# Four x tiles transposed ahead of the key weights, two more by DMA transpose, and small work moved out of the way, in a gated mix of linear attention and a token MLP

## The chip, the cores and the metric

The kernel runs on one core of a Trainium2 chip. The metric is the device time of one execution in microseconds (us); lower is better. A profiled execution also has a *span*, from its first to its last instruction; the time is the span plus about 2 us. Engine names in the profile: PE is TensorE (matmuls), PEld its weight loads, DVE is VectorE, ACT is ScalarE, POOL is GpSimd, SP is SyncE, which here only issues DMAs. A "q" behind a name means the sequencer of that engine, which issues its DMAs.

## The reference, cut to what matters

```python
x = A_x                                    # 1 x 2048 x 512, bf16
g = sigmoid((x * gate_w).sum(-1))
# a: linear attention with 32 heads of 16
q, k, v = split(x @ wqkv); pk = phi(k); pq = phi(q)      # phi(t) = t+1 if t>0 else exp(t)
kv = einsum("bhsd,bhse->bhde", pk, v);  z = pk summed over s
a = (pq @ kv) / (pq @ z) @ wo
# b: an MLP over the 2048 tokens, one for each channel
h = layernorm(x); u = gelu(h^T @ w1 + b1); b = (u @ w2 + b2)^T
out = g * a + (1 - g) * b
```

## The kernel before

A tile is 128 of the 2048 tokens; there are 16. A matmul contracts over partitions, so the key product of a tile needs x of the tile transposed (`xT`), in four chunks of 128 channels, and the four chunks of Wk. The values are never formed: each tile adds x<sup>T</sup> phi(k) to four accumulators (`gacc`), which are multiplied by Wv once at the end.

The parts that matter here, with cuts marked by `...`:

```python
load_x(nc.sync, 0, 1);  load_x(nc.scalar, 1, 1)          # x tiles 0 and 1
load_wk(nc.sync, 0);    load_wk(nc.scalar, 1)            # chunks of Wk, 128 KB each
load_wk(nc.sync, 2);    load_wk(nc.scalar, 3)
load_x(nc.sync, 2, 2);  load_x(nc.sync, 4, 4);  ...      # the other x tiles
for c in range(2, NSC):                                  # tiles 8 to 15 also transposed by DMA
    nc.sync.dma_start(out=xT[..c..], in_=X[..c..], transpose=True)
...
nc.gpsimd.dma_start(out=brow[...], ...)                  # two biases, and gw_b
...
transpose_tile(0, False); transpose_tile(1, False)       # TensorE, copied out by DVE
warm_up(2, 256)
ln_stats(0); ln_stats(1)
k_tiles((0, 1), lambda: (transpose_tile(2, False), transpose_tile(3, True)))
for t in range(2, NT):
    k_tiles((t,))                       # 4 matmuls; exp on ACT; two DVE steps give pk
    if 4 <= t + 2 < 8:
        transpose_tile(t + 2, True)     # copied out by ACT
    g_tile(t - LAG)                     # 4 matmuls into gacc, LAG = 2
    ...                                 # LayerNorm statistics of tile t on DVE
...                                     # z: 16 small matmuls
for t in range(NT):                     # second phase: first MLP product and the queries
    ...  uacc matmuls (3)  ...  q_block(t)
    if t == 1: biases()                 # transpose of 30 rows on TensorE
    if t == 4: kv_matmuls()
    if t == 8: w2_matmuls()             # 4 matmuls, copied out by DVE
```

PSUM has eight banks, all given out by one pool: four are `gacc`, the rest serve the transposes and the key products. phi takes one step on ACT (exponential) and two on DVE.

## Time and profile before

Median 170.68 us of three executions (170.6 to 170.75). The profile is of a fourth one, which took 171.28 us.

| what | value | view |
|---|---|---|
| TensorE busy | 162.9 of 169.2 us | page, part 1 |
| start of the first matmul of a key product | 4.70 us | timeline of PE |
| start of the first `gacc` | 10.45 us | timeline of PE |
| start of the first `uacc` (end of the key phase) | 37.66 us | timeline of PE |
| four matmuls of one key product or g step, back to back | 0.864 us | chain of waits |
| four transposes, warm | 0.22 us | chain of waits |
| phi of one tile on DVE, start to start | 0.92 us | timeline of DVE |

The first lines of the page: span; busy time of each engine with its share and number of instructions; then two rows in which each digit is the busy share, or the granted clock, of one fortieth of the span, in tenths.

```profile
span 169.2 us, 2119 instructions
...
PE 162.9 (96%) x814; PEld 75.0 (44%) x814; DVE 83.1 (49%) x195; ACT 58.1 (34%) x89; POOL 18.1 (11%) x36
...
PE   7889999999999999999999999999999999999991
...
PEclk9999999999999999999999999999999999999999
...
```

TensorE has nothing to gain but in the first slices. The clock row says full speed.

The timeline of TensorE in the first 14 us (start, duration, engine, line, operation, out<-in, shape, count, and in brackets the idle time before the group and what ended it):

```profile
...
1.26 2.31 PE L109 MATMUL wps<-warm 128*128 128x512 bf16 x5 [1.26 <-DVE ones_f L159]
3.44 1.04 PE L192 MATMUL pt<-ident,xs 128*128 128x128 bf16 x8
...
4.70 1.92 PE L109 MATMUL kacc<-wk_sb,xT 128*128 128x512 bf16 x6
6.96 0.59 PE L109 MATMUL kacc<-wk_sb,xT 128*128 128x512 bf16 x2 [0.34 <-DMA wk_sb<-in_A_wqkv_dram]
7.60 0.62 PE L192 MATMUL pt<-ident,xs 128*128 128x128 bf16 x8
8.51 1.04 PE L109 MATMUL kacc<-wk_sb,xT 128*128 128x512 bf16 x4 [0.29 <-DVE xT L198]
...
10.45 1.04 PE L109 MATMUL gacc<-pk,xs 128*128 128x512 bf16 x4 [0.68 <-DVE pk L206]
...
```

The key products of tiles 0 and 1 start at 4.70 us, wait for the last chunk of Wk (6.96), are followed by the transposes of tiles 2 and 3 (7.60), whose copy ends a wait (8.51), and g(0) waits for phi on DVE (10.45). The chain of waits for the same stretch (start, duration, what) links them:

```profile
...
1.73 5.18 DMA wk_sb<-in_A_wqkv_dram
...
7.60 0.64 PE pt L192 x8
...
8.26 0.60 ACT xT L196
...
9.70 0.70 DVE pk L206
...
```

The only other gap of TensorE lies in the second phase, right behind the four matmuls of W2:

```profile
...
52.49 1.03 PE L109 MATMUL wps<-wo_sb,kvbdT 128*128 128x512 bf16 x4
53.35 0.81 PE L109 MATMUL uacc<-hs,w1c 128*128 128x512 bf16 x3
54.39 1.02 PE L109 MATMUL qacc<-xT,wq_sb 128*128 128x512 bf16 x4 [0.23 <-DVE pqT L206]
...
```

The duration of a group includes about 0.16 us of pipeline behind its last matmul. Three `uacc` matmuls take 0.65 us to issue, so PE stands from 54.00 to 54.39, 0.39 us; the figure in brackets, 0.23, is the same wait counted from the modelled end of the last matmul.

### The profile page before, as it was taken

Reading aid. Unit: us, or ns where it says so; the run is one execution under the profiler, and the core shown is the slowest. Engines: PE = TensorE matmul, PEld = TensorE weight load, DVE = VectorE, ACT = ScalarE, POOL = GpSimd, SP = SyncE. Lnnn points to the kernel's source line nnn. Section 1 sums busy time; section 2 is a strip of 40 time slices with the busy share of each in tenths; the row PEclk is TensorE's granted clock in tenths of the full one; section 3 lists DMA queues with packets and bytes.
Section 4 is the critical chain, followed back from the end, with each engine's and each line's share of the span. In section 5 each row is a group of like instructions: output and inputs, shape, how many; then the busy total and the mean of one; then the engine's idle time right before and its main releaser. Section 6 shows DMA issues by size and latency. Waiting matters only on the chain.

```text
span 169.2 us, 2119 instructions
## 1 busy us (share of the span) xinstructions
PE 162.9 (96%) x814; PEld 75.0 (44%) x814; DVE 83.1 (49%) x195; ACT 58.1 (34%) x89; POOL 18.1 (11%) x36
## 2 busy tenths in 40 slices
PE   7889999999999999999999999999999999999991
PEld 3345444434544444444444444444444444444461
DVE  1679999739899868997013311316112221111121
ACT  3065767682424757222111311006111122211110
POOL 7102020200002000001522341100000000000000
PEclk9999999999999999999999999999999999999999
DMA  5999999999100000660399389971100000110001
GB/s 158 311 233 212 358 349 347 348 349 311 41 0 2 0 0 4 209 225 0 99 308 262 97 277 251 305 228 69 66 33 31 31 31 31 37 59 33 31 31 31
DMA packets 27865, 24.52 MB, mean 145 GB/s; under 512 B 5648, under 2 KB 27280, under 8 KB 27856
## 3 DMA queue, kind: packets, MB, share of 16 engines
q1 hardware_dynamic: 25984, 21.63, 43.7%
q0 software_dynamic: 1440, 2.38, 5.4%
q10 hardware_dynamic: 432, 0.39, 0.7%
q8 instruction: 6, 0.10, 0.2%
q14 instruction: 3, 0.02, 0.0%
HBM read 21.11 MB, written 2.23 MB: 138 GB/s over the span
## 4 chain that ended last, share of the span: by engine, by line
PE 92%; DMA 3%; DVE 1%; ACT 1%; ACTq 1%; issue 0%
PE yps L109 29%; PE uacc L109 28%; PE gacc L109 8%; PE qacc L109 8%; PE aps L109 8%; PE kacc L109 7%; DMA wk_sb<-in_A_wqkv_dram 3%; PE pt L192 1%; PE zacc L109 1%; ACT e L202 1%; PE denps L109 1%; PE kvps L109 1%; DVE pqT L206 0%; DVE pk L206 0%; DVE e L203 0%; ACT xT L196 0%
## 5 line engine op out<-in xcount | busy, mean ns | idle before, releaser
L109 PE MATMUL uacc<-hs,w1c 128*128 128x512 bf16 x224 | 51.3, 379 | 0.0
L109 PE MATMUL yps<-uT,w2c 128*128 128x512 bf16 (+1 forms) x238 | 51.0, 366 | 0.0
L109 PEld LDWEIGHTS <-w2c 128*128 128x128 bf16 x238 | 23.3, 98 | 25.3
L109 PEld LDWEIGHTS <-w1c 128*128 128x128 bf16 x224 | 21.6, 98 | 26.2 <-issue 0.7
L446 DVE SCALAR_TENSOR_TENSOR ot<-yps,c,a_sc 128x512 bf16<-128x512 f32 (+1 forms) x17 | 12.1, 719 | 39.5 <-PE yps L109 38.4
L431 ACT ACTIVATE a_sc<-aps,c,gg 128x512 f32<-128x512 f32 x16 | 12.2, 776 | 46.9 <-PE aps L109 36.3
L395 DVE TENSOR_TENSOR pqT<-pqT,rex 128x512 bf16<-128x512 bf16 x16 | 6.7, 424 | 28.3 <-DMA rex<-rd_dram 28.3
L308 ACT ACTIVATE uT<-uacc,bcol 128x512 bf16<-128x512 f32 x14 | 9.3, 687 | 28.6 <-PE uacc L109 28.6
L109 PE MATMUL kacc<-wk_sb,xT 128*128 128x512 bf16 x64 | 16.8, 384 | 0.7 <-DMA wk_sb<-in_A_wqkv_dram 0.3
L109 PE MATMUL gacc<-pk,xs 128*128 128x512 bf16 x64 | 16.3, 379 | 0.7 <-DVE pk L206 0.7
L109 PE MATMUL qacc<-xT,wq_sb 128*128 128x512 bf16 x64 | 16.4, 379 | 0.2 <-DVE pqT L206 0.2
L109 PE MATMUL aps<-W2sb,pqT 128*128 128x512 bf16 x64 | 16.4, 379 | 0.0
L202 ACT ACTIVATE e<-qacc 128x512 bf16<-128x512 f32 x16 | 9.6, 597 | 14.9 <-PE qacc L109 14.0
L238 ACT ACTIVATE hs<-xs,nmr,rstd 128x512 bf16<-128x512 bf16 x16 | 12.7, 804 | 0.4 <-DMA wv_sb<-in_A_wqkv_dram 0.4
L203 DVE TENSOR_SCALAR e<-e 128x512 bf16<-128x512 bf16 x32 | 9.1, 286 | 6.2 <-ACT e L202 6.0
L202 ACT ACTIVATE e<-kacc 128x512 bf16<-128x512 f32 x16 | 9.3, 597 | 7.5 <-PE kacc L109 7.5
L393 POOL DMA_DIRECT2D rex<-rd_dram x16 | 9.4, 594 | 18.0 <-DVE pqT L395 15.4
L206 DVE SCALAR_TENSOR_TENSOR pk<-kacc,e 128x512 bf16<-128x512 f32 x16 | 11.1, 692 | 0.6
L206 DVE SCALAR_TENSOR_TENSOR pqT<-qacc,e 128x512 bf16<-128x512 f32 x16 | 11.1, 691 | 0.6
L222 DVE BATCH_NORM_STATS2 stats<-xs 128x6 f32<-128x512 bf16 x16 | 10.9, 682 | 0.0
L109 PEld LDWEIGHTS <-xT 128*128 128x128 bf16 x64 | 6.2, 99 | 8.6 <-issue 1.0
L381 DVE CUSTOM_DVE_ANT_0 junk<-xs,gw_b 128x512 bf16<-128x512 bf16 x16 | 9.9, 683 | 0.0
(66 smaller groups left out, 69.1 us busy)
## 6 DMA issues: line engine op xcount, KB each, us to landing
w2c<-in_B_w_dram SPq DMA_DIRECT2D x4, 1792.0 KB, 12.2
w1c<-in_B_w_dram SPq DMA_DIRECT2D x2, 2048.0 KB, 16.9
w1c<-in_B_w_dram SPq DMA_DIRECT2D x3, 1024.0 KB, 10.2
rex<-rd_dram POOLq DMA_DIRECT2D x16, 128.0 KB, 6.7
out_dram<-ot SPq DMA_DIRECT2D x15, 128.0 KB, 1.7
xs<-in_A_x_dram SPq DMA_DIRECT2D x3, 512.0 KB, 7.6
wq_sb<-in_A_wqkv_dram SPq DMA_DIRECT2D x1, 512.0 KB, 4.3
wv_sb<-in_A_wqkv_dram SPq DMA_DIRECT2D x1, 512.0 KB, 11.1
```

What stands on the lines that cost most here:

```text
L109: nc.tensor.matmul(o, lhsT=lhsT, rhs=rhs, start=start, stop=stop, **kw)
L202: nc.scalar.activation(out=e[:], in_=acc[:], func=ACT.Exp)
L203: nc.vector.tensor_scalar(out=e[:], in0=e[:], scalar1=1.0, scalar2=PHI_EPS, op0=ALU.min, op1=ALU.add)
L206: nc.vector.scalar_tensor_tensor(out=dst, in0=acc[:], scalar=0.0, in1=e[:], op0=ALU.max, op1=ALU.add)
L222: nc.vector.bn_stats(out=stats[:], in_=xs[:, t, :])
L238: nc.scalar.activation(out=hs[:, t, :], in_=xs[:, t, :], func=ACT.Identity, scale=rstd[:, t : t + 1], bias=nmr[:, t : t + 1],)
L308: nc.scalar.activation(out=uT[:, j, :], in_=acc[:], func=ACT.Gelu_apprx_tanh, bias=bcol[:, j : j + 1])
L381: nc.vector.tensor_tensor_reduce(out=junk[:], in0=xs[:, t, :], in1=gw_b[:], scale=1.0, scalar=0.0, op0=ALU.mult, op1=ALU.add, accum_out=gp ...
L393: nc.gpsimd.dma_start(out=rex[:], in_=src.unsqueeze(1).to_broadcast([8, HEAD, SC]))
L395: nc.vector.tensor_tensor(out=seg, in0=seg, in1=rex[:], op=ALU.mult)
L431: nc.scalar.activation(out=a_sc[:], in_=aps[:], func=ACT.Identity, scale=gg[:, t : t + 1], bias=c2[:, t : t + 1],)
L446: nc.vector.scalar_tensor_tensor(out=ot[:, :W], in0=yps[:, :W], scalar=c1[:, t : t + 1], in1=a_sc[:, cs], op0=ALU.mult, op1=ALU.add,)
```

## The change

Its intent: let the first four tiles be transposed before any weight is there; then run their key products chunk by chunk, so that each chunk of Wk does four tiles' work as it lands; let the DMA transpose tiles 6 and 7; keep the queues at the start free of small loads; take W2 and its copies off DVE in the second phase. Cut to its core:

```diff
-    load_x 0, 1; load_wk 0..3; load_x 2-3, 4-7, 8-11, 12-15; then xT of 8-11 and 12-15
+    for i in range(2):
+        load_x(nc.sync, 2 * i, 1);  load_x(nc.scalar, 2 * i + 1, 1)
+    for i in range(2):
+        load_wk(nc.sync, 2 * i);    load_wk(nc.scalar, 2 * i + 1)
+    NPE = 6
+    load_x(nc.sync, 4, 2)
+    for t0, n in ((NPE, 2), (8, 4), (12, 4)):
+        load_xT(t0, n)              # DMA transpose
+        load_x(nc.sync, t0, n)
-    nc.gpsimd.dma_start(out=brow..., gw_b...)         # at the start
+    nc.gpsimd.memset(brow[:], 0.0)                    # loads issued at t == 6 of the key phase
-    warm_up(5)            # on a tile that DVE clears first
+    warm_up(6)            # on a constant that is there already
...
+    transpose_tile(0, False); transpose_tile(1, True)
+    warm_up(1, 256)
+    transpose_tile(2, False); transpose_tile(3, True)
+    for k in range(ND - 1):
+        for t in range(HEADS):                        # HEADS = 4
+            k_part(t, (k,))
+    for t in range(HEADS):
+        k_part(t, (ND - 1,))
+        if t == 1:
+            transpose_tile(HEADS, False)
+    for t in range(HEADS):
+        k_phi(t)
+    LAG = 4; LN_LAG = 3; APPLY = 9                    # LAG was 2, APPLY 6; no LN_LAG
+    for t in range(HEADS, NT):
+        k_part(t, range(ND))
+        if t + 1 < NPE:
+            transpose_tile(t + 1, True)
+        k_phi(t); g_tile(t - LAG); ...
+    for t in range(NT - LAG, NT):
+        g_tile(t)
+        if t == NT - 3:
+            for u in range(NT): z_tile(u)             # before: the last z after the last g
-        nc.tensor.transpose(pt[:, 0:n], brow[:], ident[0:n, 0:n])
+        nc.tensor.transpose(pt[:, 0:P], brow[:], ident[:])
-        if t == 8: w2_matmuls()                       # four in a row, copies on DVE
+        elif j <= NB0 + ND: w2_matmul(j - NB0 - 1)    # one after each of four later uacc, copies on ACT
```

More of the change, by code (lines that the diff above doesn't have):

```diff
@@ L92 @@
     gw_b = keep([P, D], BF16, "gw_b")
-    brow = keep([NF + NT, P], BF16, "brow")
+    brow = keep([P, P], BF16, "brow")
     bcol = keep([P, NF + NT], FP32, "bcol")
@@ L105 @@
     ones_f = keep([P, 1], FP32, "ones_f")
-    warm = keep([P, SC], BF16, "warm")
+    warm = nc.const_aps.tensor(1.0, (P, SC), BF16)
     def mm(o, lhsT, rhs, start, stop, **kw):
@@ L128, in load_wk, with load_xT @@
         q.dma_start(out=wk_sb[:, k, :], in_=wqkv_view[:, k, D : 2 * D])
-    load_x(nc.sync, 0, 1)
-    load_x(nc.scalar, 1, 1)
-    load_wk(nc.sync, 0)
-    load_wk(nc.scalar, 1)
-    load_wk(nc.sync, 2)
-    load_wk(nc.scalar, 3)
-    load_x(nc.sync, 2, 2)
-    load_x(nc.sync, 4, 4)
-    load_x(nc.sync, 8, 4)
-    load_x(nc.sync, 12, 4)
-    for c in range(2, NSC):
+    def load_xT(t0, n):
         nc.sync.dma_start(
-            out=xT[:, :, c * SC : (c + 1) * SC], in_=X[c * SC : (c + 1) * SC, :], transpose=True
+            out=xT[:, :, t0 * P : (t0 + n) * P], in_=X[t0 * P : (t0 + n) * P, :], transpose=True
         )
+    for i in range(2):
+        load_x(nc.sync, 2 * i, 1)
+        load_x(nc.scalar, 2 * i + 1, 1)
+    for i in range(2):
+        load_wk(nc.sync, 2 * i)
+        load_wk(nc.scalar, 2 * i + 1)
+    NPE = 6
[3 more added lines that the diff above has]
+        load_x(nc.sync, t0, n)
     nc.sync.dma_start(out=wq_sb[:], in_=wqkv_view[:, :, 0:D])
@@ L156 @@
             nc.sync.dma_start(out=wo_sb[:], in_=wo_view)
-    nc.vector.memset(warm[:], 0.0)
     nc.vector.memset(ones_f[:], 1.0)
@@ L172, with load_small @@
     block_mask(maskH[:].rearrange("p (a b) -> p a b", b=1), 8, 1)
-    nc.gpsimd.dma_start(out=brow[0:NF, :], in_=B_b1.rearrange("(f q) -> f q", q=P))
-    nc.gpsimd.dma_start(out=brow[NF : NF + NT, :], in_=B_b2.rearrange("(f q) -> f q", q=P))
-    nc.gpsimd.dma_start(
-        out=gw_b[:], in_=gate_w.rearrange("(o d) -> o d", o=1).to_broadcast([P, D])
-    )
+    nc.gpsimd.memset(brow[:], 0.0)
+    def load_small():
+        nc.gpsimd.dma_start(out=brow[0:NF, :], in_=B_b1.rearrange("(f q) -> f q", q=P))
+        nc.gpsimd.dma_start(out=brow[NF : NF + NT, :], in_=B_b2.rearrange("(f q) -> f q", q=P))
+        nc.gpsimd.dma_start(
+            out=gw_b[:], in_=gate_w.rearrange("(o d) -> o d", o=1).to_broadcast([P, D])
+        )
     wps = bank("wps")
@@ L208, in phi, with k_part, k_phi @@
         )
-    def k_tiles(ts, between=None):
-        accs = [bank("kacc") for _ in ts]
-        for k in range(ND):
-            for t, acc in zip(ts, accs):
-                mm(acc[:], xT[:, k, t * P : (t + 1) * P], wk_sb[:, k, :], k == 0, k == ND - 1)
-        if between:
-            between()
-        for t, acc in zip(ts, accs):
-            phi(pk[:, t, :], acc)
+    kaccs = {}
+    def k_part(t, ks):
+        if t not in kaccs:
+            kaccs[t] = bank("kacc")
+        for k in ks:
+            mm(
+                kaccs[t][:], xT[:, k, t * P : (t + 1) * P], wk_sb[:, k, :],
+                k == 0, k == ND - 1,
+            )
+    def k_phi(t):
+        phi(pk[:, t, :], kaccs.pop(t))
     def ln_stats(t):
@@ L241, in ln_apply @@
         )
-    gacc = [bank("gacc") for _ in range(ND)]
+    gacc = []
     def g_tile(t):
+        if not gacc:
+            gacc.extend(bank("gacc") for _ in range(ND))
         for k in range(ND):
@@ L264, in z_tile, with ln_step @@
         )
-    transpose_tile(0, False)
-    transpose_tile(1, False)
-    warm_up(2, 256)
-    ln_stats(0)
-    ln_stats(1)
-    k_tiles((0, 1), lambda: (transpose_tile(2, False), transpose_tile(3, True)))
-    LAG = 2
-    APPLY = 6
-    for t in range(2, NT):
-        k_tiles((t,))
-        if 4 <= t + 2 < 8:
-            transpose_tile(t + 2, True)
+    def ln_step(u):
+        ln_stats(u)
+        if u % TPC == TPC - 1:
+            ln_rstd(u // TPC)
+    HEADS = 4
+    transpose_tile(0, False)
+    transpose_tile(1, True)
+    warm_up(1, 256)
+    transpose_tile(2, False)
+    transpose_tile(3, True)
+    ln_step(0)
+    ln_step(1)
+    for k in range(ND - 1):
[7 more added lines that the diff above has]
+        k_phi(t)
+    LAG = 4
+    LN_LAG = 3
+    APPLY = 9
+    for t in range(HEADS, NT):
+        k_part(t, range(ND))
+        if t + 1 < NPE:
+            transpose_tile(t + 1, True)
+        k_phi(t)
         g_tile(t - LAG)
+        if t > LAG:
+            ln_step(t - LN_LAG)
+        if t == TPC - 1 + LN_LAG:
+            load_small()
         if t >= APPLY:
             ln_apply(t - APPLY)
-        if t < 12:
-            ln_stats(t)
-            if t % TPC == TPC - 1:
-                ln_rstd(t // TPC)
-        if t % TPC == 1 and t > TPC:
-            ln_shift(t // TPC - 1)
-    zacc = bank("zacc")
-    g_tile(NT - 2)
-    for t in range(NT - 1):
-        z_tile(t)
-    g_tile(NT - 1)
-    z_tile(NT - 1)
-    ln_apply(10)
-    ln_apply(11)
+        if t % TPC == 0 and t >= 2 * TPC:
+            ln_shift(t // TPC - 2)
+    zacc = bank("zacc")
+    for t in range(NT - LAG, NT):
+        g_tile(t)
+        if t == NT - 3:
+            for u in range(NT):
+                z_tile(u)
+    ln_shift(2)
+    ln_apply(NT - APPLY)
     nc.vector.tensor_copy(out=zhi[:], in_=zacc[:])
@@ L313, in biases @@
         pt = bank("pt", BF16)
-        n = NF + NT
-        nc.tensor.transpose(pt[:, 0:n], brow[:], ident[0:n, 0:n])
-        nc.vector.tensor_copy(out=bcol[:], in_=pt[:, 0:n])
+        nc.tensor.transpose(pt[:, 0:P], brow[:], ident[:])
+        nc.vector.tensor_copy(out=bcol[:], in_=pt[:, 0 : NF + NT])
     def kv_matmuls():
@@ L337, in kv_matmuls, with w2_matmul @@
         )
-    def w2_matmuls():
-        for j in range(ND):
-            wps2 = bank("wps2")
-            mm(wps2[:], kvbdT[:, j, :], wo_sb[:, j, :], True, True)
-            nc.vector.tensor_copy(out=W2sb[:, j, :], in_=wps2[:])
+    def w2_matmul(j):
+        wps2 = bank("wps2")
+        mm(wps2[:], kvbdT[:, j, :], wo_sb[:, j, :], True, True)
+        nc.scalar.activation(out=W2sb[:, j, :], in_=wps2[:], func=ACT.Copy)
     def den_matmuls():
@@ L361 @@
         q_block(t)
-        if 2 <= t < 6:
-            ln_stats(t + 10)
-        if t == 5:
-            ln_rstd(3)
-        if t == 7:
+        if 2 <= t < 2 + LN_LAG:
+            ln_step(NT - LN_LAG + t - 2)
+        if t == 3 + LN_LAG:
             ln_shift(3)
-        if 8 <= t < 12:
-            ln_apply(t + 4)
+        if 1 <= t < 5 or 7 <= t < 11:
+            ln_apply(t + 7 if t < 5 else t + 5)
         if t == 1:
@@ L373 @@
             kv_matmuls()
-        if t == 8:
-            w2_matmuls()
     for jj in range(NB0):
@@ L412 @@
             rden_chain()
+        elif j <= NB0 + ND:
+            w2_matmul(j - NB0 - 1)
         if jj == FB - 1 or j == NF - 1:
```

## The prediction

> **What bounds the kernel now.** TensorE. The page gives it 162.9 of 169.2 us busy, 92% of the chain that ended last, at granted clock 1.00. Its exposed time lies at the start. The PE timeline has 1.26 us before the first matmul, 2.3 us of warm-up, then waits. The chain runs ACT's DMA issues, then a 5.18 us landing of the last Wk chunk (6.92 us), then the two last contractions of tiles 0 and 1, eight transposes, the copy of tile 3, an exponential, and phi on DVE. gacc starts at 10.45 us. From there to the first uacc (37.73 us) PE never idles by the windows table. Later only one gap shows: 0.39 us at 54.0 (uacc ends after its 0.65 us of issue, qacc starts at 54.39; 0.23 us by the modelled ends), behind phi on DVE, just after the four W2 matmuls; four W2 copies then take DVE 2.47 us.
>
> **Costs, from the trace.** Four contractions of a tile, or one g step: 0.864 us. Four warm transposes: 0.22 us. DVE copy 0.42, ACT copy 0.59, phi 0.92 per tile on DVE, LayerNorm statistics 0.80.
>
> **Removed.** Eight TensorE transposes (tiles 6, 7): 0.44 us, and their ACT copies. The serial stretch in which PE waits for copies and phi: contractions of four tiles now fill it. The W2 gap: 0.39 us. At the end of the K phase the wait for pk of tile 15 (about 0.1 us, and a z matmul standing alone, 0.32 us against 0.065).
>
> **Added.** 256 KB more of x (DMA transpose) and two x tiles queued ahead of Wk. Wk thus lands as items three and four of each queue. Today the third items land at 5.99 (SP) and 6.92 us (ACT), but 15 of their 16 completions come by 5.33 and 5.83. One laggard remains, perhaps because the small loads on the Pool queue start then; the change moves those away. My estimate: Wk0 at 5.3, the last Wk chunk near 6.5 us.
>
> **New critical path.** T0 and T1 from 3.45 us, T2 and T3 to about 5.3 us, at the cold pace seen today (107 ns a step until about 5.1 us; "TensorE: Matmul & The Clock Gate", Part 1, calls it half rate until a busy window has passed). T3's copy on ACT ends near 6.1 us, behind table load and T1's copy. Then sixteen contractions to 8.9, T4, its copy, tile 4 from 9.35, T5, g(0) from 10.4, whose fourth bank waits for T5's copy (0.2 us). Afterwards no wait: DVE needs about 1.72 us a tile, PE 1.73, and a lag of four tiles absorbs the rest. First uacc near 35.0 instead of 37.73: 2.75 us. With W2: 3.15 us. Everything on this sum is critical, since PE is the bound. Transposed tiles 6, 7 should land by 10 us, needed at 13; later weights have over 5 us of slack.
>
> **Prediction.** 167.5 us, range 166.9 to 168.4 (-1.9%). Faster by over 2% (below 167.3): 0.40; within 2%: 0.58; slower: 0.02.
>
> **What would show it.** First four-tile contraction near 5.4 us, tile 4's near 9.4, first uacc near 35.0; no PE gap behind phi after 13 us, none near the old 54 us; 24 instead of 32 x transposes; the phases from uacc on unchanged in length, except for W2's matmuls moved among uacc.
>
> **What would make it wrong.** Wk later than 6.5 us with the laggard still there (+0.5 us or more); the clock still cold during the first contractions (427 instead of 216 ns each); DMA transposes stalling the SP queue (today's first took 7.7 us to issue), so that tiles 6, 7 or the x loads behind them come late; DVE falling behind before tile 15; or copies faster than assumed, which would push it under 167.

## The result, and the profile after

The changed kernel takes 168.59 us (median of six, 168.3 to 168.79); the kernel before took 170.72 in the same rounds (170.6 to 171.32). The ratio is 0.9865, with a 95% interval of 0.9844 to 0.9886. The prediction of 167.5 us, with a range up to 168.4, was too low by 1.1 us; its most likely class, within 2%, was right.

The page of a changed execution of 168.46 us:

```profile
span 166.4 us, 2105 instructions
...
PE 161.7 (97%) x806; PEld 74.9 (45%) x806; DVE 80.2 (48%) x190; ACT 59.0 (35%) x91; POOL 18.2 (11%) x37
...
PE   7999999999999999999999999999999999999992
...
```

The timeline of TensorE at the start:

```profile
...
0.84 2.72 PE L109 MATMUL wps<-const-bfloat16-1.0 128*128 128x512 bf16 x6 [0.84 <-PEq L490]
3.62 1.03 PE L197 MATMUL pt<-ident,xs 128*128 128x128 bf16 x8
...
4.66 0.96 PE L197 MATMUL pt<-ident,xs 128*128 128x128 bf16 x8
6.03 3.18 PE L109 MATMUL kacc<-wk_sb,xT 128*128 128x512 bf16 x14 [0.41 <-DMA wk_sb<-in_A_wqkv_dram]
9.05 0.39 PE L197 MATMUL pt<-ident,xs 128*128 128x128 bf16 x4
9.27 1.72 PE L109 MATMUL kacc<-wk_sb,xT 128*128 128x512 bf16 x6
10.83 0.39 PE L197 MATMUL pt<-ident,xs 128*128 128x128 bf16 x4
11.05 1.23 PE L109 MATMUL gacc<-pk,xs 128*128 128x512 bf16 x4
...
```

The chain of waits of the same stretch:

```profile
...
1.72 4.26 DMA wk_sb<-in_A_wqkv_dram
...
6.03 3.18 PE kacc L109 x14
9.21 0.24 PE pt L197 x4
...
9.47 0.43 DVE xT L203
...
9.95 1.04 PE kacc L109 x4
...
11.21 0.65 PE gacc L109 x3
...
11.90 0.38 PE gacc L109
...
```

The new order is there, and almost nothing is idle once it has begun. But the sixteen key matmuls of the four tiles begin at 6.03 us, when Wk chunk 0 has landed. Two small waits are left: tile 4's key product starts at 9.95, though the matmuls before it have been issued by 9.70, because DVE has to copy the transposed tile (9.47 to 9.90); and the fourth matmul of g(0) starts at 11.90 instead of 11.70, because its bank is still being read by the copy of tile 5.

In the second phase the gap is gone (the same two kinds of matmul, back to back):

```profile
...
50.94 1.03 PE L109 MATMUL qacc<-xT,wq_sb 128*128 128x512 bf16 x4
51.80 0.81 PE L109 MATMUL uacc<-hs,w1c 128*128 128x512 bf16 x3
52.45 1.03 PE L109 MATMUL qacc<-xT,wq_sb 128*128 128x512 bf16 x4
...
```

From profile to profile the change brings 2.8 us of span:

| stretch | before | after | gain |
|---|---|---|---|
| start to the first `uacc` | 37.66 | 35.64 | 2.02 |
| gap behind W2 | 0.39 | 0 | 0.39 |
| transpose of the biases, from the end of the `qacc` before it to the `uacc` after it | 0.22 | 0.06 | 0.16 |
| start of the last DVE step to the end of the span | 3.38 | 3.22 | 0.16 |

The third row I had not foreseen at all. On the timeline, before and after (the four `qacc` matmuls take 0.865 us to issue, so they end at 40.69 and 38.66):

```profile
...
39.83 1.03 PE L109 MATMUL qacc<-xT,wq_sb 128*128 128x512 bf16 x4
40.79 0.18 PE L315 MATMUL pt<-ident,brow 30*128 30x30 bf16 x1
40.91 0.82 PE L109 MATMUL uacc<-hs,w1c 128*128 128x512 bf16 x3
...
```

```profile
...
37.80 1.03 PE L109 MATMUL qacc<-xT,wq_sb 128*128 128x512 bf16 x4
38.66 0.22 PE L343 MATMUL pt<-ident,brow 128*128 128x128 bf16 x1
38.72 0.81 PE L109 MATMUL uacc<-hs,w1c 128*128 128x512 bf16 x3
...
```

Here a full 128 by 128 transpose, mostly of zeros, costs TensorE less than one of 30 rows: 0.06 us in all thirteen traces of the changed kernel and its variants, 0.21 to 0.22 in all five of the kernel before. The weight loads (PEld) show where the difference lies: that of the 30 rows starts at 40.79, when the `qacc` matmuls before it have all been issued (40.69), while the full one starts at 38.45, under the last of them. Why the smaller load is not taken earlier was not tested. The fourth row is seen in every trace looked at, too (3.38 to 3.39 us in the five before, 3.20 to 3.22 in the changed kernel and most variants, 3.31 in e_pe8); why the tail behind the last compute instruction is shorter I have not tried to find out.

### The profile page after: what moved, and what is told of

It is laid out like the page before. It is cut to its first block, busy times and chain, and to the rows that moved or that the text cites. A ratio compares the mean times of both kernels' runs of the same rounds, so it can differ in the third digit from the quotient of the medians.

```text
span 166.4 us, 2105 instructions
## 1 busy us (share of the span) xinstructions
PE 161.7 (97%) x806; PEld 74.9 (45%) x806; DVE 80.2 (48%) x190; ACT 59.0 (35%) x91; POOL 18.2 (11%) x37
## 4 chain that ended last, share of the span: by engine, by line
PE 94%; DMA 3%; DVE 1%; SPq 0%; issue 0%
PE uacc L109 29%; PE yps L109 29%; PE gacc L109 8%; PE qacc L109 8%; PE aps L109 8%; PE kacc L109 8%; DMA wk_sb<-in_A_wqkv_dram 3%; PE zacc L109 1%; PE denps L109 1%; PE kvps L109 1%; PE wps L109 1%; SPq L125 0%; DVE ot L471 0%; PE pt L197 0%; DVE xT L203 0%
## 5 line engine op out<-in xcount | busy, mean ns | idle before, releaser
L109 PE MATMUL uacc<-hs,w1c 128*128 128x512 bf16 x224 | 52.0, 379 | 0.0
L109 PE MATMUL kacc<-wk_sb,xT 128*128 128x512 bf16 x64 | 16.1, 379 | 0.5 <-DMA wk_sb<-in_A_wqkv_dram 0.4
```

Source lines behind the costliest of these rows:

```text
L109: nc.tensor.matmul(o, lhsT=lhsT, rhs=rhs, start=start, stop=stop, **kw)
```

## The experiments

Sixteen runs followed, five of them repeats of an unaltered kernel. All gave correct results but one that was wrong on purpose. "First key matmul", "first phi" (its first step on DVE), "pk(15)" (end of tile 15's phi on DVE) and "first uacc" are read from the timelines, in us.

| run | first key matmul | first phi | pk(15) | first uacc | median us | ratio to before (95%) |
|---|---|---|---|---|---|---|
| changed kernel | 6.03 | 9.81 | 33.50 | 35.64 | 168.59 | 0.9865 (0.9844-0.9886) |
| after_again | 5.92 | 9.70 | 33.37 | 35.53 | 168.38 | 0.9877 (0.9836-0.9919) |
| e_nowk0 | 5.10 | 9.10 | 32.78 | 34.93 | 168.22 | 0.9841 (0.9814-0.9868) |
| e_small_back | 5.85 | 9.63 | 33.28 | 35.46 | 168.77 | 0.9878 (0.9857-0.99) |
| e_w2_back | 6.14 | 9.92 | 33.60 | 35.75 | 169.07 | 0.9897 (0.9875-0.992) |
| e_bytile | 5.99 | 9.60 | 33.28 | 35.40 | 168.23 | 0.9844 (0.9828-0.986) |
| e_fast1 | 6.01 | 10.09 | 33.78 | 35.88 | 168.67 | 0.9869 (0.9854-0.9885) |
| e_fast2 | 4.92 | 10.17 | 33.86 | 35.96 | 168.82 | 0.9882 (0.9864-0.9901) |
| e_fast1_ln | 5.96 | 10.14 | 32.78 | 35.22 | 168.80 | 0.9878 (0.9852-0.9903) |
| e_npe4 | 6.14 | 9.77 | 33.46 | 35.55 | 168.37 | 0.9854 (0.983-0.9878) |
| e_best | 6.02 | 9.00 | 32.69 | 34.78 | 167.68 | 0.9812 (0.9787-0.9837) |
| e_pe8 | 6.03 | 9.81 | 33.80 | 36.09 | 169.23 | 0.99 (0.9877-0.9923) |
| e_best2 | 4.82 | 8.72 | 32.42 | 34.52 | 167.34 | 0.9784 (0.9766-0.9801) |

### The yardstick again

No edit.

> The changed kernel unaltered, as the yardstick of this chip. Expected span 166.4 us, time near 168.6 us, the first contraction at about 6.0 us (behind Wk chunk 0), tile 4's at about 9.95, the first uacc at about 35.65. If the slowest of the 16 completions of each early load again comes about 0.5 us behind the other 15, the laggard belongs to the chip and not to one execution.

The trace agrees with the first within 0.15 us in every column of the table. The trace also records the 16 completions of each load; the Trainium skill ("DMA: Bandwidth & Descriptors", Why a DMA increments its semaphore by 16) says that only all 16 mean that the data has landed, and this agrees: the first contraction starts 0.04 us after the sixteenth. Here Wk chunk 0 had 15 of its completions at 5.61 and the last at 5.88, against 5.50 and 5.99 in the first trace. So there is a laggard, but its size changes: over the eleven traces that load x and Wk in this order, the last completion of chunk 0 came 0.01 to 0.49 us behind the fifteenth, and yet the chunk landed at 5.76 to 6.10 us in all of them. One of the six executions took 170.62 us (span 168.5), which widens this run's interval; I have no trace of it.

### Is it the weights that hold the start?

```diff
+                warm if t < HEADS and k == 0 else wk_sb[:, k, :],   # wrong result on purpose
-                wk_sb[:, k, :],
```

> Wrong result on purpose: the first chunk's contractions of tiles 0 to 3 read a constant instead of Wk chunk 0, so they wait for no load of weights. Theory (late weights are what my forecast mis-sized): they start near 4.9 us, behind the copies of the tiles; chunk 1 then starts with its own load at 6.17, tile 4's contraction comes 0.5 us earlier (9.45), the time falls by 0.5 us to about 168.1. Rival (the transposed copies or the cold clock hold the start): tile 4's contraction moves by less than 0.2 us.

In the trace the key matmuls start at 5.10 and the first `uacc` comes 0.60 us before the yardstick's. The late weights are therefore worth 0.6 us in that execution, as the theory says. (With the weights out of the way, the fourth of the early matmuls still starts only at 5.95 us, behind the copy of its tile.) Its timed median gained less, 0.16 us, and its executions spread from 167.34 to 168.66. A probable reason, argued and not shown, is the clock: in the traced execution the step from one transpose to the next fell from 107 to 56 ns at about 4.7 us, so the early matmuls ran at full pace; in others that step comes later (see below).

### Do the small loads make the laggard?

```diff
+    load_small()            # at the start again
     wps = bank("wps")
-        if t == TPC - 1 + LN_LAG:
-            load_small()
```

> Only the three small loads on the Pool queue go back to the start. The prediction's guess (they make the laggard): the slowest completion of each Wk chunk lags by about 1.1 us instead of 0.5, chunk 0 lands near 6.5, time +0.5 us. Rival (the laggard is there without them, as the trace of the changed kernel suggests): chunk 0 lands within 0.15 us of 5.99, time within 0.15 us.

Chunk 0 had 15 completions at 5.58 and the last at 5.81 us, no worse than without the small loads. With the changed kernel's own trace, in which the laggard is 0.49 us without them, this refutes what the prediction built on its guess, that moving them rids Wk of the laggard. The median is 0.4 us above the yardstick's and 0.2 above the changed kernel's first one. The ratio equals the yardstick's only because the yardstick's mean holds the one execution of 170.62 us. So the timing does not settle whether moving the loads is worth anything; the trace shows no loss up to the first `uacc`, though the transposed tiles 6 and 7 landed at 11.44 us instead of 8.51 (they are needed at 13.66).

### The W2 product back in its place

```diff
+        if t == 8: w2_matmuls()          # copies on DVE
-        elif j <= NB0 + ND: w2_matmul(j - NB0 - 1)
```

> Only the W2 product goes back to its old place, with its copies on DVE. Theory: the gap of 0.39 us behind phi comes back near 52 us, time +0.4 us (about 169.0). Rival (the gap came from the late shift of the whole DVE queue before, not from W2): no gap, time within 0.15 us.

The wait came back; the median is 0.5 us above the changed kernel's first one and 0.7 above the yardstick's of the same rounds:

```profile
...
52.30 1.02 PE L109 MATMUL qacc<-xT,wq_sb 128*128 128x512 bf16 x4 [0.23 <-DVE pqT L211]
...
```

From the first `uacc` to `den` it is 30.03 us against 28.77 in the changed kernel: 0.86 us of W2's own matmuls, which only moved, and 0.40 us of gap. That part of the prediction held. The run moves the place of the product and the engine of its copies together. In the trace of the kernel before, the copies begin at 54.25 us, behind the phi step (begun at 53.65) that ended the wait, so the four matmuls in a row are the likelier cause; this is read from the trace and not tested apart.

### Tiles 6 and 7 on TensorE again

```diff
-    NPE = 6
-    load_x(nc.sync, 4, 2); then (xT, x) of 6-7, 8-11, 12-15
+    NPE = 8
+    load_x(nc.sync, 4, 4); then (xT, x) of 8-11, 12-15
```

> The changed kernel with tiles 6 and 7 transposed on TensorE again, as before. Theory (the two groups of four transposes lie on the critical path): first uacc 0.44 us later than in the changed kernel, near 36.0, time +0.44. Rival (the DVE row of 23.7 us bounds the phase by now, with 0.35 us of slack against TensorE): only what exceeds that slack is lost or, with the copies on ACT delaying phi, more than 0.44.

The first `uacc` came 0.45 us after the changed kernel's, with the same start of the key matmuls: the 0.44 us of transposes were all on the critical path. By ratio the loss is 0.35%, 0.6 us, against the first rounds of the changed kernel, and 0.4 us against the yardstick; the intervals overlap, so it is the trace that shows it.

### Chunk by chunk or tile by tile?

```diff
-    for k in range(ND - 1): for t in range(HEADS): k_part(t, (k,))     # and the last chunk
+    for t in range(HEADS):
+        k_part(t, range(ND))
+        if t == 2: transpose_tile(HEADS, False)
```

> The first four tiles are contracted tile by tile instead of chunk by chunk. Theory A (what the intent of the change says: only chunk by chunk hides the arrival of the weights): TensorE waits inside tile 0 for chunks 1 to 3, the last lands near 6.8 us; 0.25 us of waiting more, but tile 4's transpose copy is now hidden (0.25 us less), so tile 4's contraction starts within 0.15 us of 9.9 and the time is the same within 0.2 us. Theory B (the chunk order carries most of the gain): tile 4's contraction 0.5 us or more later, time +0.5 us.

Theory A holds, and a little more: the first `uacc` comes at 35.40 and the median is 168.23, not slower than chunk by chunk. By the time that chunk 0 is there, the others follow within 0.9 us, so little is left to hide. The order of the sixteen matmuls is therefore not what carries the gain here (e_best below shows where order does count: when it decides the start of phi). That the four tiles transposed ahead are is what remains, but no run tests it alone.

### Removing the last two waits on TensorE

```diff
+    for k in range(ND):
+        if k == 2:
+            transpose_tile(HEADS, False); transpose_tile(HEADS + 1, True)
+        for t in range(HEADS): k_part(t, (k,))
     ...
+        if t == HEADS: continue            # tiles 4 and 5 contracted, then g(0), g(1)
+        if t == HEADS + 1: g_tile(0)
```

> Meant to be faster: tiles 4 and 5 are transposed ahead of the third chunk, and tile 5 is contracted before the first g step, so the waits for the copies of tiles 4 and 5 (0.25 and 0.2 us) have work in front of them. Theory (these two waits are all that is left between the first contraction and the first uacc): first uacc 0.45 us earlier than in the changed kernel (35.1 against 35.55), time -0.45 us. Rival (DVE, which takes phi of tiles 0 to 5 in one row, becomes the wait): uacc moves by less than 0.15 us.

This was my idea of a faster kernel, and it was not faster. The two waits did go, and a new one stood at the end of the phase:

```profile
...
32.44 1.04 PE L109 MATMUL zacc<-pk,zsel 128*32 128x512 bf16 x15
33.84 0.38 PE L109 MATMUL zacc<-pk,zsel 128*32 128x512 bf16 x1 [0.35 <-DVE pk L211]
34.15 1.90 PE L109 MATMUL gacc<-pk,xs 128*128 128x512 bf16 x8
...
```

The last z matmul waits for pk of tile 15. DVE is the reason. In the changed kernel its timeline begins the phis at 9.81, behind the copy of tile 4, and from there DVE never rests:

```profile
...
9.47 0.42 DVE L203 COPY xT<-pt 128x512 bf16<-128x512 bf16 x1 [2.11 <-PE pt L197]
9.81 0.28 DVE L208 TENSOR_SCALAR e<-e 128x512 bf16<-128x512 bf16 x1
10.13 0.69 DVE L211 SCALAR_TENSOR_TENSOR pk<-kacc,e 128x512 bf16<-128x512 f32 x1
...
```

"Never rests" means no idle time above 60 ns before any DVE instruction of the row. The table shows it without any timeline: pk(15) minus the first phi is 23.65 to 23.70 us in eleven of the thirteen traces of the changed kernel and its variants, whatever TensorE does. The exceptions are the next run, made to shorten it, and the one with eight transposes (23.99). By then TensorE and DVE end the phase nearly together: in the changed kernel pk(15) was there at 33.50 and the last z matmul needed it at about 33.9. My reordering delayed the first phi by 0.28 us and advanced TensorE by about as much, and that used up the slack of about 0.4 us.

```diff
+ the same, and Wk chunk 0 second on its queue, x tile 2 third; tiles 0, 1, 3 contracted first
```

> The order above, and the queues reordered so that Wk chunk 0 is second on its queue and x tile 2 third: chunk 0 lands near 4.2 instead of 5.9 us, contractions of tiles 0, 1 and 3 start near 5.0, tile 2 joins after its load at 5.9. Theory (the landing of the first 0.75 MB is what sets the start): tile 4's contraction near 9.6 against 9.9 in the run above, uacc 0.35 us earlier still, time -0.8 us against the changed kernel. Rival (total bytes set it, the order does not matter): within 0.15 us of the run above.

The key matmuls started at 4.92 us, 1.1 us earlier, and nothing was gained. The first `uacc` came even later, for the first phi was no earlier (10.17). The early matmuls also ran at half pace:

```profile
...
4.92 1.51 PE L109 MATMUL kacc<-wk_sb,xT 128*128 128x512 bf16 x3
...
```

The second and third started 0.43 and 0.47 us after the one before and not 0.216, and the step reached full pace only near 6.7 us. The Trainium skill ("TensorE: Matmul & The Clock Gate", Part 1) describes it: the array starts at half rate and is let go after a busy window of about 3.4 us whose phase is not tied to the kernel's start. The traces agree that the moment differs from execution to execution, though the earliest comes sooner than a full window after the first matmul: that matmul is at 0.84 us in the changed kernel and its variants, and the step from 427 to 216 ns (or 107 to 56 for transposes) fell at about 3.5 us in one trace (e_bytile), 4.1 (e_best), 4.7 (e_nowk0), 5.3 (changed kernel) and 6.7 (e_fast2). All this time the page's clock row reads 9, full.

### Is it really DVE?

```diff
-    LN_LAG = 3
+    LN_LAG = 4              # one tile's statistics leave the key phase
```

This is on top of e_fast1. The same number also sets when the small loads are issued, one tile later.

> The reordered kernel that moved the wait of 0.35 us to the last z matmul, with one tile's LayerNorm statistics and one rstd input (0.95 us of DVE) taken out of the K phase and done four q blocks later. Theory (DVE, never idle from its first phi on, is the second bound: in eight traces pk of tile 15 ends 23.65 to 23.69 us after the first phi begins): pk of tile 15 comes 0.95 us earlier, the wait is gone, the first uacc is near 35.2 instead of 35.88, time about 168.1. Rival (the reordering itself costs time on TensorE, DVE is only busy): uacc stays within 0.15 us of 35.88.

As the theory has it, pk(15) minus the first phi fell to 22.64, the wait for pk went away, and the first `uacc` came at 35.22. But the time stayed. The wait had moved on:

```profile
...
36.61 1.02 PE L109 MATMUL qacc<-xT,wq_sb 128*128 128x512 bf16 x4 [0.58 <-DVE zhl L326]
...
```

```profile
...
34.92 0.16 DVE L241 SCALAR_TENSOR_TENSOR nmr<-mv,rstd 128x4 f32<-128x4 f32 x1 [1.12 <-POOL rstd L237]
...
```

With the later statistics, the small power function on POOL (1.01 us for 128 by 4) ends later too. DVE, in order, stands 1.12 us in front of the shift that needs it, and the first query product of the next phase, which needs a bank that DVE frees, comes late by 0.74 us (35.87, where the three `uacc` matmuls are issued, to 36.61; 0.58 by the modelled end). So DVE as the second bound is shown by the trace, and the time shows that easing it in this way gives the gain back at the next place.

### Fewer transposes

```diff
-    NPE = 6; load_x 4-5; then (xT, x) of 6-7, 8-11, 12-15
+    NPE = 4; load_xT(4, 2); load_xT(6, 2); load_x(nc.sync, 4, 4); then (xT, x) of 8-11, 12-15
```

No tile is transposed behind the first four, so no copy of one stands in front of the phis on DVE. With the chunk order kept:

> The changed kernel with tiles 4 and 5 brought by DMA transpose as well, so only four tiles are transposed on TensorE; the chunk order stays. Removed: two times 0.22 us of transposes and the waits for their copies (0.25 and 0.2 us). Theory: tile 4's contraction directly behind the first sixteen (9.5 us), g(0) near 10.5 behind phi, which starts at 9.5 and ends pk of tile 15 at 33.2; first uacc near 34.9, time -0.7 us against the changed kernel (about 167.9). Rival (256 KB more on the queue bring the transposed tiles too late, or slow Wk down): TensorE waits at tile 4 or 6.

Little of it came: the first `uacc` is at 35.55 against 35.64 in the changed kernel (34.9 expected), the median 168.37 against 168.59 and the yardstick's 168.38. The key matmuls began at 6.14, tile 4's followed without a wait, g(0) waited for phi (0.23 us by the modelled ends, 0.38 from the last issue), and the end of the phase waited for DVE: the first phi was no earlier than in the changed kernel (9.77), and the z matmuls, 1.05 us in the fast case, took

```profile
...
32.58 1.31 PE L109 MATMUL zacc<-pk,zsel 128*32 128x512 bf16 x16
...
```

Then chunks 2 and 3 tile by tile, so that tile 0 is finished first:

```diff
+    for k in range(2):
+        for t in range(HEADS): k_part(t, (k,))
+    for t in range(HEADS): k_part(t, (2, 3))
```

> As the run above, and chunks 2 and 3 are contracted tile by tile, so that the first four tiles end one after the other and phi starts 0.55 us earlier on DVE. Theory: no wait on TensorE between the first contraction and the first uacc, 28.7 us in all: uacc near 34.75, time near 167.7, the fastest of all. Rival (DVE start does not matter): same as the run above within 0.1 us.

Now it fits. The first phi is at 9.00, the timeline names no wait of TensorE between 6.02 and the first `uacc` at 34.78, and the time is 167.68 us:

```profile
...
6.02 4.48 PE L109 MATMUL kacc<-wk_sb,xT 128*128 128x512 bf16 x20 [1.03 <-DMA wk_sb<-in_A_wqkv_dram]
10.33 1.03 PE L109 MATMUL gacc<-pk,xs 128*128 128x512 bf16 x4
...
```

The twenty key matmuls of five tiles run in one row, and g(0) follows at once. The rival fell: the first `uacc` lies 0.77 us before that of the kernel above (0.12 of it because Wk chunk 0 landed earlier in this trace), and the median 0.69 us, from an order of eight matmuls that TensorE itself does not feel.

### Where the executions of the kernel before differ

No edit; five traces in all.

> The kernel before, unaltered, for a second trace. Its executions fall in two groups (170.4 and 171.0 to 171.4 us; spans 168.4 and 168.9 to 169.3). Theory: the trace that the forecast rested on (span 169.2) is of the longer group, whose Wk chunk 3 lands 0.5 to 1 us later because the slowest completion lags by 1.1 us. If this trace has a span near 168.4, its last Wk chunk should land near 6.3 us instead of 6.92 and its gacc start near 9.8 instead of 10.45. Rival (the difference lies in a later phase): chunk 3 lands within 0.2 us of 6.92 at either span.

> The kernel before, unaltered, a third trace. Theory: what differs between its executions (spans 168.2 to 169.4 us) lies ahead of gacc, in the landing of the last Wk chunk (6.92 at span 169.2, 6.53 at 169.0) and of x tiles 2 and 3: at a span of 168.4 gacc starts near 9.7 us, and the rest from gacc to the end is 158.75 us within 0.15 in every trace. Rival: the rest varies by as much as the start.

> The same once more, a fourth trace: gacc start plus 158.75 us is the span, within 0.15 us (theory); or not (rival).

> The same once more, a fifth trace: gacc start plus 158.75 us is the span, within 0.15 us (theory); or not (rival).

| trace | time | span | last Wk chunk | x tiles 2, 3 | first gacc | span minus first gacc |
|---|---|---|---|---|---|---|
| the one of the prediction | 171.28 | 169.2 | 6.92 | 7.55 | 10.45 | 158.75 |
| b_again1 | 171.08 | 169.0 | 6.53 | 7.07 | 10.27 | 158.73 |
| b_again2 | 171.31 | 169.2 | 6.78 | 7.32 | 10.52 | 158.68 |
| b_again3 | 170.97 | 168.9 | 6.01 | 7.28 | 10.18 | 158.72 |
| b_again4 | 171.02 | 169.0 | 6.72 | 7.22 | 10.24 | 158.76 |

What varies is the start, through the landing of the first loads; behind the first `gacc` the five agree within 0.08 us. "Last Wk chunk" is the one that landed last, chunk 2 in b_again1 and b_again2 and chunk 3 in the others. My expectation for the first of these runs, that the last Wk chunk alone decides, fell: in b_again3 it landed at 6.01, and then x tiles 2 and 3 were what TensorE waited for. No trace caught an execution of 170.4 to 170.7 us, so that their start is earlier by the missing half microsecond follows from the sum and is not seen.

### The best kernel, once more with the weights earlier

The queue order of e_fast2 on top of e_best.

> The fastest kernel so far with the queues reordered (Wk chunk 0 second on its queue, x tile 2 third). Theory: with neither the copies of tiles 4 and 5 nor DVE in the way, an earlier start is no longer given back: contractions of tiles 0, 1 and 3 from 4.9 us, phi on DVE from 8.5, first uacc near 34.4 instead of 34.78, time near 167.3. Rival (the matmuls started early run at half pace, 427 instead of 216 ns, and win nothing): within 0.15 us of 167.65.

The median is 167.34 us and the ratio 0.9784; the interval ends at 0.9801, so whether the gain passes 2% stays just open. What brought nothing in e_fast2 brings about 0.3 us here (167.68 to 167.34, in other rounds, with overlapping intervals; 0.26 at the first `uacc`), as the first phi now moves with it (8.72). In this trace the half-rate time was also over sooner, at 4.5 us against 6.7 in e_fast2; but no execution of e_fast2 was under 168.75 us and none of this kernel over 167.57, so the chance of one trace does not explain the difference. It is the fastest kernel, ahead of both that were compared. The first `uacc`, at 34.52, is 0.1 us later than expected.

## Why the prediction was wrong

The number is a sum: 170.68, minus 2.75 for the start, minus 0.39 for W2. Point by point:

- **The bound was right.** TensorE is 97% busy after, and in the traces what is put back on its critical path moves everything behind it: e_pe8 gives back 0.45 us for two groups of transposes (0.44 forecast), e_w2_back 0.40 for the gap (0.39 forecast).
- **The step that failed first: "My estimate: Wk0 at 5.3".** It landed at 5.99, and at 5.76 to 6.10 in the ten other traces with the same order of loads up to Wk. The forecast had put the first contraction at 5.4 us; it is at 6.03. I had taken the fifteenth completion of the third load on the SP queue in the old trace (5.33) and dropped the sixteenth (5.99), on the guess that the small loads made it late. The laggard is there without them (0.49 us), so the guess fell. But it is not the whole of the error: the fifteenth completion itself came at 5.50, and at up to 6.05 in the other traces. Nor was the old sixteenth a safe number: the same load of the kernel before ended at 5.99, 6.53, 6.78, 5.83 and 6.50 in five traces, so that 5.99 twice is partly chance. What makes the third load of a queue land near 6 us stays open; put second on its queue, chunk 0 landed at 4.04 and 4.25 (e_fast2, e_best2). The last chunk was late as well, at 6.87 instead of "near 6.5". e_nowk0 shows what the wait for weights is worth, 0.6 us in the trace. So the start brought 2.02 us and not 2.75; 0.63 of the 0.73 missing are this one term, and 0.07 come from 37.73, a start in the chain of waits, where the timeline has 37.66.
- **The second: the sum was taken from the wrong base.** All its terms were read from an execution of 171.28 us, and subtracted from a median of 170.68 us. The five traces show that executions of this kernel differ just in the start, which is where the forecast gains lay, so the inflated start was counted as gain. That is 0.60 us. From 171.28 the same sum gives 168.1. The arithmetic is certain; that the faster executions differ in the start alone is seen between spans of 168.9 and 169.2 us and not below. And the median itself moved: the kernel before had 170.72 in the rounds of the result and 170.82 to 171.17 in the later ones, so the measured gain was 2.1 us there and 2.6 in the yardstick's rounds.
- **Missed on the other side:** 0.16 us from the transpose of the biases and 0.16 behind the last compute step. With these the account closes: 167.5 + 0.60 + 0.73 - 0.32 = 168.5, against 168.46 for the profiled execution and a median of 168.59.
- **Right in mechanism and size:** the waits for the copies of tiles 4 and 5 (forecast 0.2 each, found 0.25 and 0.2), 24 instead of 32 transposes of x, no gap near the old 54 us, the transposed tiles 6 and 7 in time (landed at 8.5 us, needed at about 14).
- **"DVE needs about 1.72 us a tile, PE 1.73, and a lag of four tiles absorbs the rest" was right for this kernel and hid how near the limit it was.** No wait appears, but the slack left is about 0.4 us, and e_fast1 spent it.
- **The clock** did not hurt the changed kernel in its trace, because it waits for the weights until 6.03 us and the half-rate time was over at 5.3; in the trace of e_fast1_ln it lasted until 6.2. It may be a reason why starting earlier pays less than it seems.

## What to carry to other kernels

Subtract a forecast gain from the time of the execution that was profiled, not from the median of others, and find out first in which phase executions of the same kernel differ. A load has landed when its last completion has; do not drop the laggard on a guess about its cause, and do not take a landing time from a single trace. And when the waits of one engine are removed, look for an engine with an unbroken row of work under it: here the distance from the first phi to the last was 23.7 us in eleven of thirteen traces, and the clearly faster variants (e_best, e_best2) are those that also began that row earlier.

## What the Trainium skill lacked or had wrong

- "TensorE: Matmul & The Clock Gate", Part 1, puts the change to full rate at around 4 us of activity, give or take 500 ns from run to run. Here it came 2.7 us (e_bytile) to 5.9 us (e_fast2) after the first matmul at 0.84 us. The 500 ns do not cover a spread of 3.2 us. The page's free-running window of 3.4 us is about as wide, but in three traces the change came sooner than that after the first matmul (2.7 us in e_bytile, 3.0 in e_npe4, 3.3 in e_pe8), which leaves no room for one full busy window. The same part does warn that the number of cold matmuls changes from run to run.
- "DMA: Bandwidth & Descriptors", Latency and other measured facts, says that DMA engines 7 and 15 are usually slower and guesses at a cause specific to the Pool queue's path. Here the last of 16 completions of chunk 0 lagged by 0.01 to 0.49 us in ten traces with no Pool load in flight, and by 0.23 us with the small Pool loads back. The trace does not name the engine, so this does not contradict the page; it shows a laggard that needs no Pool load.
- The same page has no figure for how far such landings differ between executions: the last Wk chunk of one unaltered kernel landed between 6.01 and 6.92 us in five traces.
- No page that I read says that a transpose of a 30-row tile can cost TensorE more than a full one: 0.22 us against 0.06 here, from the end of the matmuls before it to the start of those after it.
